# Filler matmuls ahead of the first k^T v, and block 1's q transposed by VectorE

One TensorE program on Trainium2, with a change in two parts. In the opening, six matmuls without a purpose of their own ("filler") are put ahead of the first k^T v, and a second group of filler grows from 7 to 12. At the border between block 0 and block 1, the transposing of block 1's q moves from TensorE to VectorE.

## Chip, cores and metric

One core of one Trainium2 chip. The metric is device time of one execution in microseconds (us). All executions quoted are of the fast state, but for the one of e5, whose state is not known. "Clock" is the granted TensorE clock averaged over a run, 1.000 being full speed; the record counts the time before the first rise as 1.000 too (in the kernel before its first entry is the rise at 22.21 us, and the stretch from 0 to 22.2 reads 1.00). Microseconds read from a trace are of one profiled run of each kernel.

## The reference

```python
def _attn_ref(q, k, v, g_norm):              # q, k, v: (8, 8, 576, 64) float32
    kv = np.einsum('bhsd,bhse->bhde', k, v)  # "k^T v"
    out = np.einsum('bhsd,bhde->bhse', q, kv)  # "q times kv"
    rms = np.sqrt(np.mean(out * out, axis=-1, keepdims=True) + 1e-06)
    return out / rms * g_norm

def _moe_ref(x, w_gate, w_val, w_out):       # x: (4608, 512), d_ff = 1536
    g = x @ w_gate
    silu = g * (1.0 / (1.0 + np.exp(-g)))
    return silu * (x @ w_val) @ w_out

# reference: x = attention output, heads joined, (B*S, H*D); result = _moe_ref(x, ...)
```

## The kernel before

The kernel takes the 4608 tokens in 9 blocks of 512. Each block runs k^T v, q times kv, the norm, up (gate and value), h = silu(g) * value, and down. From block 1 on the large products are computed from sums of sub-blocks that VectorE and GpSimd prepare (`h_sums`, `turn_t`: fewer matmuls, more adding). A scheduler orders each engine's instructions; `tc.issue_after(x)` asks that what is inside be issued behind x.

```python
def load_q(self, i):
    if self.n >= TURNED:                 # TURNED = 3: later blocks load q in quarters
        self.load_quarters(i)
        return
    if self.n == 1:
        tiles = [t_tile().rearrange("p a b -> p (a b)") for _ in range(2)]
    # ... (cut: other blocks' tiles, and the loads)

def turn_q(self, i, pools=None):
    # ...
    if self.n >= TURNED:                 # VectorE transposes
        nc.vector.transpose(out=..., in_=self.q[i])
        return
    for t in (2 * i, 2 * i + 1):         # TensorE transposes, 4 matmuls a tile
        # ... (cut)
        for j in range(NS):
            nc.tensor.transpose(ps[:, j], self.q[t][:, j], ident)

def first(self):                         # block 0
    self.turn_q(0, (b_psum, c_psum))
    self.first_kv()                      # k^T v
    self.product(0)                      # q times kv, first half
    with tc.issue_after(self.multiplied.ins):
        self.turn_q(1, (b_psum, c_psum))
    # ... (cut)
        self.product(1, (b_psum, a_psum))
    self.warm()                          # filler, bridges VectorE's root and scale
    self.root(0, 2)
    self.scale(0)
    # ... (cut)
    self.turn_x(0)
    self.scale(1)

def warm(self):
    ps = c_psum.tile([P, NS, P], F32, name="c")
    for _ in range(7):
        nc.tensor.matmul(ps, lhsT=ident, rhs=self.qt[:, 3], start=True, stop=True)

# the start of the program
blocks[0].load_q(0)
blocks[0].load_first_kv()
blocks[0].load_q(1)
load_weights(4)                          # first four pieces of the weights, 512 KB each
squared, scaled = blocks[0].first()
```

Of the kernel before, what the change touches and what calls it, by code (L numbers as in the profile page):

```python
# [8 lines left out]
F32 = mybir.dt.float32  # L9
# [5 lines left out]
P = 128  # L15
# [3 lines left out]
def kernel(  # L19
# [41 lines left out]
    nc = tc.nc  # L61
# [5 lines left out]
    BLK = P * T  # L67
# [7 lines left out]
    LD = 2 * KT * D  # L75
# [4 lines left out]
    def pool(name, bufs, **kw):  # L80
        return ctx.enter_context(tc.tile_pool(name=name, bufs=bufs, **kw))

    consts = pool("consts", 1)
    ld_pool = pool("ld", 4)
# [14 lines left out]
    ident = consts.tile([P, P], F32, name="ident")  # L99
# [15 lines left out]
    def ring():  # L115

        return r_pool.tile([P, 4, BLK], F32, name="r")

    class Words:
# [12 lines left out]
        def __init__(self, src, shape):  # L132
            self.raw = ld_pool.tile([P, LD], U32, name="ld")[:, 0 : 2 * BLK]
            dst = self.raw.rearrange("p (a b) -> p a b", a=shape[0])
            self.sent = nc.sync.dma_start(out=dst, in_=src)
            self.shape = shape
            self.begun = False
# [55 lines left out]
    class Att:  # L193


        def __init__(self, n):
            self.n = n

            self.cut, half = divmod(n, 2)
            self.split = half * D  # L200
            self.ps, self.z = {}, None
            self.q, self.k, self.v, self.room = [], {}, {}, None
            self.halves = []

        def parts(self, t):

            n, first = self.n, P * t - D * self.n
            if t < self.cut:
                return [(n - 1, S + first, 0, P)]
            if t == self.cut and self.split:  # L210
                return [(n - 1, S - D, 0, D), (n, 0, D, P)]
            return [(n, first, 0, P)]
# [73 lines left out]
            self.q.append(ld)  # L286

        def load_q(self, i):
            if self.n >= TURNED:
                self.load_quarters(i)  # L290
                return
            if self.n == 1:
                tiles = [t_tile().rearrange("p a b -> p (a b)") for _ in range(2)]
            else:
                ld = ld_pool.tile([P, LD], F32, name="ld")
                tiles = [ld[:, 0:BLK], ld[:, BLK : 2 * BLK]]
            for t in range(2):
                tile_ = tiles[t].rearrange("p (h d) -> p h d", h=H)
                for b, s0, p0, p1 in self.parts(2 * i + t):
                    nc.sync.dma_start(  # L300
                        out=tile_[p0:p1], in_=q[b, :, s0 : s0 + p1 - p0, :].rearrange("h p d -> p h d")
                    )
                self.q.append(tile_.rearrange("p (j u) d -> p j (u d)", u=2))
# [21 lines left out]
        def turn_q(self, i, pools=None):  # L325

            if i == 0:
                self.qt = ring().rearrange("p j (t c) -> p t j c", t=T)
            if self.n >= TURNED:
                to = self.qt[:, :, 2 * i : 2 * i + 2].rearrange("p t j c -> p j t c")  # L330
                nc.vector.transpose(out=to.rearrange("p j t c -> p (j t c)"), in_=self.q[i])
                return
            for t in (2 * i, 2 * i + 1):
                pool = pools[t % 2] if pools else m_psum
                ps = pool.tile([P, NS, P], F32, name=pool.name[0])
                for j in range(NS):
                    nc.tensor.transpose(ps[:, j], self.q[t][:, j], ident)
                if t % 2 if self.n == 0 else t:
                    self.copied_q = nc.scalar.copy(out=self.qt[:, t], in_=ps)
                else:  # L340
                    nc.vector.tensor_copy(out=self.qt[:, t], in_=ps)
# [115 lines left out]

        def first(self):
            self.turn_q(0, (b_psum, c_psum))
            self.first_kv()  # L460
            self.product(0)
            with tc.issue_after(self.multiplied.ins):
                self.turn_q(1, (b_psum, c_psum))

            with tc.issue_after(self.copied_q.ins), tc.issue_after(self.summed.ins):
                begun = words[pieces[0]].begin()
            with tc.issue_after(begun.ins):
                self.product(1, (b_psum, a_psum))
            self.warm()
            self.root(0, 2)  # L470
            self.scale(0)
            with tc.issue_after(self.squared.ins), tc.issue_after(self.scaled.ins):
                weights(1)
            self.turn_x(0)
            self.scale(1)
            return self.squared, self.scaled

        def warm(self):

            ps = c_psum.tile([P, NS, P], F32, name="c")  # L480
            for _ in range(7):
                nc.tensor.matmul(ps, lhsT=ident, rhs=self.qt[:, 3], start=True, stop=True)

        def turn(self):
            for i in range(2):
# [42 lines left out]
    TURNED = 3  # L528
# [267 lines left out]
    def t_tile(key=None):  # L796

        stream.held.append(key)
        return t_pool.tile([P, 2, 2 * P], F32, name="t")
# [114 lines left out]
    class Ffn:  # L914
# [49 lines left out]
        def down(self, nxt):  # L964

            down = self.down_
            fill = nxt.steps() if nxt else {}
            for p in (1, 6, 5, 7, 2, 4, 3) if 5 in fill else (1, 5, 6, 7, 2, 4, 3):
                if p == 1:
                    down.turn_t(7, self.ended)  # L970
                if p == 6:
                    down.turn_t(4, nxt.halves[0] if nxt and nxt.n >= TURNED else None)
                down.multiply(p)
                self.make(12)
                if p == 5 and self.n == DEEP - 1:
                    for i in range(2):
                        self.loads(i)
                if p in fill:
                    fill[p]()
                if p == 1:  # L980
                    down.turn_s3()



# [37 lines left out]
    def weights(upto):  # L1022
        nonlocal rounded
        while rounded < min(upto, len(pieces)):
            load_weights(rounded + 4)
            round_w(*pieces[rounded])
            rounded += 1
# [14 lines left out]
    for n in range(NB):  # L1042
        ffn = Ffn(n, blocks[n])
        nxt = blocks[n + 1] if n + 1 < NB else None
# [84 lines left out]
```

## Time and profile before

| kernel before | value |
|---|---|
| time, median of 3 runs | 1037.47 us (1037.41 to 1038.24) |
| span of the profiled run | 1036.2 us |
| TensorE busy | 1014.5 us (98%) |
| VectorE busy | 700.4 us (68%) |
| clock of the profiled run | 1.000 |

TensorE is the bound. So the questions are what TensorE waits for, in which stretch, and at which clock its matmuls run. The lines for that stand in the prediction below. In a timeline, a line has the start, the length, the engine, the line of the kernel, the operation with its tiles, how many records it joins (x72), and in brackets the idle time before it with what ended it.

### The profile page before, as it was taken

How to read it: one execution, taken by the hardware profiler on the slowest of the kernel's cores; microseconds unless marked ns; L12 is line 12 of the kernel's file. 1: busy time of each engine (PE TensorE's matmuls, PEld its weight loads, DVE VectorE, ACT ScalarE, POOL GpSimd, SP SyncE). 2: the span in 40 equal slices, each digit the busy share in tenths (PEclk: the TensorE clock that was granted, in tenths of full speed). 3: DMA queues.
4: the chain of work that ended last, by engine and by line, in shares of the span. 5: the costliest groups of instructions: out<-in, count | busy, mean ns of one | idle time of the engine just before them, and what ended most of it. 6: DMA issues, size and time to landing. Idle time of an engine off the chain costs nothing.

```text
span 1036.2 us, 21446 instructions
## 1 busy us (share of the span) xinstructions
PE 1014.5 (98%) x8586; PEld 904.9 (87%) x8586; DVE 700.4 (68%) x1184; ACT 231.4 (22%) x362; POOL 369.5 (36%) x280
## 2 busy tenths in 40 slices
PE   5999999999999999999999999999999999999998
PEld 4544688778899989998999899988999899989997
DVE  2999596898556856575666666684668566856661
ACT  2665111222212211212111111211212111212110
POOL 0000443435025621563146305640455136512670
PEclk9999999999999999999999999999999999999999
DMA  7689604775468556865686368736862766066601
GB/s 214 200 262 273 140 1 127 186 203 138 130 190 245 120 113 200 240 158 87 195 245 181 61 203 233 212 50 178 247 192 50 171 200 194 22 153 213 191 30 42
DMA packets 247876, 168.15 MB, mean 162 GB/s; under 512 B 124640, under 2 KB 215904, under 8 KB 247776
## 3 DMA queue, kind: packets, MB, share of 16 engines
q1 hardware_dynamic: 221280, 163.36, 56.7%
q10 hardware_dynamic: 26432, 3.41, 2.1%
q8 instruction: 68, 1.11, 0.4%
q14 instruction: 32, 0.26, 0.1%
q0 software_dynamic: 64, 0.00, 0.0%
HBM read 138.02 MB, written 22.41 MB: 155 GB/s over the span
## 4 chain that ended last, share of the span: by engine, by line
PE 91%; DVE 5%; DMA 2%; issue 1%; ACT 1%; POOL 0%; SPq 0%; DVEq 0%; ACTq 0%; POOLq 0%
PE b L700 26%; PE b L551 20%; PE c L700 13%; PE c L551 10%; PE a L700 6%; PE a L551 5%; PE b L994 4%; PE c L994 4%; PE m L316 2%; PE m L357 1%; DVE xi L112 1%; DMA h<-in_v_dram 1%; DVE r L112 1%; DVE t L111 1%; DVE h L112 0%
## 5 line engine op out<-in xcount | busy, mean ns | idle before, releaser
L111 POOL TENSOR_TENSOR r<-r 128x256 f32<-128x256 f32 (+1 forms) x105 | 110.9, 1063 | 308.2 <-DVE r L111 234.3
L111 DVE TENSOR_TENSOR r<-b,r 128x512 f32<-128x512 f32 (+1 forms) x273 | 162.0, 606 | 63.9 <-PE b L700 59.3
L112 POOL TENSOR_TENSOR t<-wo 128x512 f32<-128x512 f32 x81 | 115.6, 1453 | 191.9 <-DVE wo L111 105.4
L111 DVE TENSOR_TENSOR r<-c,r 128x512 f32<-128x512 f32 (+1 forms) x179 | 108.4, 617 | 95.5 <-PE c L700 56.1
L700 PE MATMUL b<-x,t 128*128 128x128 f32 x1092 | 151.0, 275 | 0.0
L700 PEld LDWEIGHTS b<-x,t 128*128 128x128 f32 x1092 | 136.5, 192 | 0.6 <-DVE r L111 0.2
L111 DVE TENSOR_TENSOR r<-a,r 128x512 f32<-128x512 f32 (+1 forms) x99 | 62.5, 631 | 108.7 <-PE a L551 65.8
L113 POOL TENSOR_TENSOR h<-r 128x1024 f32<-128x1024 f32 (+1 forms) x40 | 81.7, 2059 | 88.7 <-DVE r L111 75.6
L700 PE MATMUL c<-xi,t 128*128 128x128 f32 x840 | 112.2, 275 | 0.4 <-DVE xi L111 0.4
L700 PEld LDWEIGHTS c<-xi,t 128*128 128x128 f32 x840 | 102.8, 192 | 0.5 <-DVE xi L111 0.5
L551 PE MATMUL b<-wo,h 128*128 128x256 f32 x432 | 99.4, 382 | 0.1
L551 PE MATMUL b<-t,h 128*128 128x256 f32 x432 | 96.9, 381 | 0.0
L551 PEld LDWEIGHTS b<-t,h 128*128 128x128 f32 x432 | 81.3, 190 | 11.3 <-issue 0.2
L551 PEld LDWEIGHTS b<-wo,h 128*128 128x128 f32 x432 | 79.9, 190 | 12.7 <-DVE h L113 2.5
L714 ACT COPY r<-b 128x512 f32<-128x512 f32 x63 | 36.9, 586 | 212.0 <-PE b L700 200.1
L700 PE MATMUL b<-xi,t 128*128 128x128 f32 x588 | 79.7, 276 | 0.0
L700 PEld LDWEIGHTS b<-xi,t 128*128 128x128 f32 x588 | 72.4, 192 | 0.0
L700 PE MATMUL b<-x,wg 128*128 128x128 f32 x336 | 52.7, 279 | 0.2 <-DVE x L112 0.2
L700 PE MATMUL b<-x,wv 128*128 128x128 f32 x336 | 51.3, 275 | 0.0
L551 PE MATMUL c<-t,s 128*128 128x256 f32 x216 | 48.3, 380 | 0.0
L551 PE MATMUL a<-wo,h 128*128 128x256 f32 x216 | 48.3, 379 | 0.0
L551 PE MATMUL c<-wo,h 128*128 128x256 f32 x216 | 48.1, 379 | 0.0
(136 smaller groups left out, 1579.1 us busy)
## 6 DMA issues: line engine op xcount, KB each, us to landing
t<-w SPq DMA_DIRECT2D x336, 256.0 KB, 3.4
out_dram<-r SPq DMA_DIRECT2D x17, 512.0 KB, 3.1
ld<-in_k_dram SPq DMA_DIRECT2D x26, 288.0 KB, 4.8
ld<-in_v_dram SPq DMA_DIRECT2D x26, 288.0 KB, 5.6
ld<-in_moe_w_gate_dram SPq DMA_DIRECT2D x12, 512.0 KB, 4.7
ld<-in_moe_w_val_dram SPq DMA_DIRECT2D x12, 512.0 KB, 4.6
ld<-in_moe_w_out_dram SPq DMA_DIRECT2D x12, 512.0 KB, 5.1
w<-t SPq DMA_DIRECT2D x18, 256.0 KB, 2.3
```

Source lines behind the costliest of these rows:

```text
L111: add = lambda e, o, a, b: e.tensor_tensor(out=o, in0=a, in1=b, op=OP.add)
L112: sub = lambda e, o, a, b: e.tensor_tensor(out=o, in0=a, in1=b, op=OP.subtract)
L113: mul = lambda e, o, a, b: e.tensor_tensor(out=o, in0=a, in1=b, op=OP.mult)
L316: nc.tensor.matmul(self.kv_ps[r][u * D : (u + 1) * D, g, :], lhsT=k[:, u, c, :], rhs=v[:, u, c, :], start=(c == 0), stop=(c == KT - 1),)
L357: self.multiplied = nc.tensor.matmul(self.ps[i][u][p : p + D, t, j, :], lhsT=self.qt[rows, 2 * i + t, j, p : p + D], rhs=kvs[b % 3][rows, ...
L551: nc.tensor.matmul(banks[e][:, e], lhsT=lhsT, rhs=rhs, start=first and i == 0 and (e == 0 or banks[0] is not banks[1]), stop=i == self.ste ...
L700: nc.tensor.matmul(ps[:, i, f], lhsT=self.weight(o, p, f), rhs=self.operand(o, p), start=first and (i, f) == (0, 0), stop=True, skip_group ...
L714: nc.scalar.copy(out=dst, in_=ps)
L994: nc.tensor.matmul(t, lhsT=w[f // 2][:, i, P * (f % 2) : P * (f % 2 + 1)], rhs=x[:, i, of], start=(i == 0), stop=(i == NS - 1),)
```

## The change

The intent: keep TensorE busy while it waits for k and v, so that it is at full clock when k^T v begins (in the kernel before the clock rose only at 22.21 us, behind k^T v); and take 16 transposes from TensorE at a place where VectorE has time.

```diff
         def __init__(self, n):
+            self.quarters = n == 1 or n >= TURNED
...
         def load_q(self, i):
-            if self.n >= TURNED:
+            if self.quarters:
                 self.load_quarters(i)
                 return
-            if self.n == 1:
-                tiles = [t_tile().rearrange("p a b -> p (a b)") for _ in range(2)]
-            else:
-                ld = ld_pool.tile([P, LD], F32, name="ld")
-                tiles = [ld[:, 0:BLK], ld[:, BLK : 2 * BLK]]
+            ld = ld_pool.tile([P, LD], F32, name="ld")
+            tiles = [ld[:, 0:BLK], ld[:, BLK : 2 * BLK]]
...
-            if self.n >= TURNED:
+            if self.quarters:
                 to = self.qt[:, :, 2 * i : 2 * i + 2].rearrange("p t j c -> p j t c")
-                nc.vector.transpose(out=to.rearrange("p j t c -> p (j t c)"), in_=self.q[i])
+                self.q_turned = nc.vector.transpose(out=to.rearrange("p j t c -> p (j t c)"), in_=self.q[i])
...
         def first(self):
             self.turn_q(0, (b_psum, c_psum))
+            self.warm(6)
             self.first_kv()
             self.product(0)
...
-            self.warm()
+            self.warm(12)
...
-        def warm(self):
+        def warm(self, count):
             ps = c_psum.tile([P, NS, P], F32, name="c")
-            for _ in range(7):
-                nc.tensor.matmul(ps, lhsT=ident, rhs=self.qt[:, 3], start=True, stop=True)
+            for _ in range(count):
+                nc.tensor.matmul(ps, lhsT=ident, rhs=self.qt[:, 0], start=True, stop=True)
...
-                down.multiply(p)
+                with tc.issue_after(nxt.multiplied.ins) if self.n == 0 and p in (5, 6) else ExitStack():
+                    down.multiply(p)
...
                 if p == 1:
-                    down.turn_s3()
+                    with tc.issue_after(nxt.q_turned.ins) if self.n == 0 else ExitStack():
+                        down.turn_s3()
```

## The prediction

> **What bounds the kernel now.** I read the page first, then the waits of TensorE, then the timeline and the chain in the two places that the change touches: the opening (0 to 40 us) and the border of block 0 and block 1 (115 to 126 us).
>
> The busy slices and the waits of TensorE (total, times, longest):
> ```profile
> PE   5999999999999999999999999999999999999998
> ...
> PE b L551 <- ACT r L601: 5.7, 4, 2.3
> PE m L247 <- DMA h<-in_v_dram: 5.6, 2, 4.8
> PE b L337 <- DMA ld<-in_q_dram: 4.2, 1, 4.2
> ```
> TensorE is the bound nearly everywhere: only the first slice is half empty. So a microsecond counts only if it leaves TensorE's own row. The listed waits come to some 17 us of 1036; those on k, v and q belong to the opening.
>
> The opening, timeline of TensorE (start, length, then what it is; L247 is k^T v, L357 q times kv, L482 the existing filler, L404 the turning of x):
> ```profile
> 5.76 1.11 PE L337 MATMUL c<-ident,ld 128*128 128x128 f32 x4 [0.43 <-DMA ld<-in_q_dram]
> 11.72 2.40 PE L247 MATMUL m<-h 64*64 64x64 f32 x72 [4.84 <-DMA h<-in_v_dram]
> 14.91 2.41 PE L247 MATMUL m<-h 64*64 64x64 f32 x72 [0.79 <-DMA h<-in_v_dram]
> 17.92 1.99 PE L357 MATMUL m<-kv,r 64*64 64x64 f32 x64 [0.60 <-DVE kv L111]
> ...
> 23.11 6.28 PE L482 MATMUL c<-r,ident 128*128 128x512 f32 x14
> 29.65 1.06 PE L404 MATMUL m<-ident,r 128*128 128x128 f32 x8 [0.27 <-DVE r L113]
> ```
> k^T v waits for v, which lands in two halves (11.6 and 14.8 us). The filler of 7 matmuls (14 records) bridges the wait for VectorE's root and scale; TensorE goes on at 29.65, 0.27 us after it, released by VectorE. From 39.8 us on it has no gap until block 1.
>
> The same 72 records of k^T v for block 1, and the turning of block 1's q, at 115 us:
> ```profile
> 115.39 1.28 PE L316 MATMUL m<-xi 64*64 64x64 f32 x72
> 116.49 1.25 PE L316 MATMUL m<-ld 64*64 64x64 f32 x72
> 117.67 0.65 PE L337 MATMUL c<-ident,t 128*128 128x128 f32 x4
> 118.16 0.60 PE L337 MATMUL b<-ident,t 128*128 128x128 f32 x4
> 118.59 0.60 PE L337 MATMUL c<-ident,t 128*128 128x128 f32 x4
> 119.03 0.60 PE L337 MATMUL b<-ident,t 128*128 128x128 f32 x4
> 119.47 1.89 PE L551 MATMUL b<-wo,h 128*128 128x256 f32 x8
> ```
> 72 records take 1.1 us here start to start against 2.4 us in the opening, so TensorE runs at half speed there. The records of L357 shorten from 0.31 to 0.22 us at 22.2 us; until then all is slow.
>
> VectorE beside it, and its own transposes of later blocks:
> ```profile
> 115.57 0.69 DVE L113 TENSOR_TENSOR h<-h,c 128x512 f32<-128x512 f32 x1 [6.18 <-PE c L994]
> 116.29 1.76 DVE L111 TENSOR_TENSOR s<-h 128x1536 f32<-128x1536 f32 x1
> 118.09 1.76 DVE L112 TENSOR_TENSOR h<-s,h 128x1536 f32<-128x1536 f32 x1
> ...
> 124.85 1.76 DVE L112 TENSOR_TENSOR h<-h 128x1536 f32<-128x1536 f32 x1 [4.41 <-PE b L551]
> ...
> L331 DVE STREAM_TRANSPOSE r<-ld x12: 1221/1230/1235, 348.6 to 889.7; 128x1024 f32<-128x1024 f32 x12
> ```
> After the sums of h VectorE has 4.41 us free: room for two transposes of 1.23 us.
>
> [...]records of 0.31 us until 22.2 us, 4.3 us after the last gap ended at 17.92, 0.22 us from then on. The page's granted clock reads 1.00 all the while[...]. [...]the quarters move 128 B runs. In the trace later blocks issue such a load every 0.5 us and it lands after 2.0 us (median). [...]at 133.9 us a 128x512 subtract of VectorE beside GpSimd takes 1.76 us, alone 0.68.
>
> **The change, part by part.**
>
> Part 1, block 1's q. Removed from TensorE: 16 transposes, 117.67 to 119.47 = 1.80 us. They stand on the path: TensorE has no gap from 39.8 to 180 us. Added on VectorE: 2 x 1.23 us after the sums of h, 119.85 to 122.2, less a copy of 0.69 that goes. TensorE now goes from k^T v (117.67) straight to the first product of down, 5.2 us, and reaches q times kv at 122.85; VectorE is done at 122.2. The built order puts four matmuls of the second q tile early in it, so both turns are needed, with 0.65 us of slack. The loads: 5 become 32, still 1 MB. Today q's loads issue from 98.8 and land by 111.6. Now they need tiles of the weights' loads, the last read at 101.7, and issue at 0.5 us each: 101 + 16 + 2 = about 119, before the second turn at 121. What follows (block 1's up, where VectorE holds TensorE four times, 5.7 us) starts from events of TensorE, so the shift should carry to the end. After the border the built order of every engine is unchanged. Worth: -1.80.
>
> Part 2, the opening. Six filler matmuls start when the first q copy is done and the transposes are issued, about 6.7 us. One costs 0.86 us at full clock (L482: 0.43 per record, two records), 1.72 at half. The clock rises 4.3 us after work starts by the trace[...]; I take 11.5 us. By then (11.5 - 6.7)/1.72 = 2.8 are done, the other 3.2 take 2.75 us: they end at 14.25. So k^T v starts 2.5 us late, but at full speed: 14.25 + 1.1, then + 1.1 (v's second half is there at 14.8): last end 16.65 against 17.32. Then + 0.6 (kv's copy and add), product(0) 0.95 instead of 1.9, 8 transposes 0.87 instead of 1.9: 19.1 against 21.8. VectorE's chain to x comes with it: about 27.1 instead of 29.5, 2.4 us earlier. But the second filler grows from 7 to 12. In the built order one of them goes ahead of product(1) and 11 behind it: product(1) ends about 20.9, plus 11 x 0.858 = 9.44, makes 30.35. TensorE would then turn x 0.7 us later than today, with x long ready. Of the small waits behind it (0.27, 0.34, 0.20 us) some part goes: full-width work starts perhaps 0.3 us later. Worth: +0.3[...]. The sum of weights that VectorE does earlier is worth nothing, because TensorE is the bound from 40 to 115 us.
>
> Part 3, possible delay of the turns, +0.2 on average (rival B).
>
> Sum: 1037.47 - 1.80 + 0.30 + 0.20 = 1036.2 us.
>
> **Rivals.**
> A. The second filler is no bound, because x is ready only at about 30 us after all (weights of 512 KB landing at 17.8 and 20.5 us, ScalarE's work on them between). Then the opening gains what VectorE's chain gains, up to 2 us: 1034 to 1035. For it: somebody chose 12. Against it: in the chain of waits the span from 21.8 to 29.5 is ScalarE and VectorE alone, no DMA, and it starts with transposes that come 2.7 us earlier.
> B. The turns come late. GpSimd makes nine tiles of wo; today five, then it waits 4.01 us for tiles that hold q, so it is quiet during the first sum of h. Now it isn't stopped, and may meet the sums: each meeting costs VectorE up to 1.1 us. Or the 32 small loads, queued behind k and v loads that take 7 us to land, come at 122 instead of 119. Each would make TensorE wait 0.5 to 1.5 us at q times kv: 1036.7 to 1037.7. Against it: VectorE's weights end about 2 us earlier, so GpSimd starts its nine earlier too.
> C. The gain at the border is swallowed in block 1 by VectorE (busy 19.7 of 20 us at 200 to 240). Then 1037.5 to 1038. Against it: VectorE's work there begins on TensorE's results, and at 160 to 180 it is busy 14 of 20 us.
> D. The filler doesn't lift the clock and runs all cold to 17 us: k^T v late by 5 us, time 1039 or more. Against it: a busy TensorE lifted it once already.
>
> **Range and chances.** [...]B costs up to 1.5, A gives up to 2; runs of one kernel differ by 0.8. Range 1034.6 to 1037.6. Two per cent is 20.7 us; nothing here is of that size, so within 2% nearly surely.
>
> **What would show it.** Right: no transposes by TensorE at 117 us, two of VectorE before q times kv, and no gap of TensorE ahead of it; records of k^T v in block 0 near 0.22 us; a fall to short records between 10 and 14 us; the second filler ending at 30 to 31 us with no wait behind it. Wrong: a wait of TensorE on VectorE's transpose or on q at 123 us (B); a wait after the second filler (A); block 1's wait on ScalarE grown by what was saved (C); k^T v records of 0.31 us (D).

## The result, and the profile after

| | before | after |
|---|---|---|
| time, median | 1037.76 us (1037.41 to 1038.24, 4 runs) | 1044.01 us (1043.26 to 1044.77, 4 runs) |
| ratio | | 1.006 (1.0042 to 1.0077) |
| span of the profiled run | 1036.2 us | 1042.7 us |
| clock, each run | 1.000 (profiled) | 0.997 (profiled), 0.995, 0.995, 0.995 |

Ratios here are the mean time of one kernel's fast runs over that of the other's of the same rounds, so they are not quite the ratio of the medians quoted. The changed kernel is some 6 us slower, within 2% but far outside the predicted range. I followed single TensorE instructions through both traces and noted how much later each starts in the changed kernel. The difference is +4.29 us when the full-width products begin (39.76 us before, 44.05 after), falls to +3.50 behind the border of block 0 and 1, grows by about 2.6 in block 1 and by about 0.6 later.

**The opening.** The waits of TensorE in the changed kernel have a new entry (total, times, longest):

```profile
PE b L550 <- ACT r L600: 6.6, 4, 2.7
...
PE m L355 <- issue: 2.2, 1, 2.2
...
PE m L355 <- DVE r L329: 0.3, 1, 0.3
```

"issue" says that the engine waited for nothing that the profile knows. Its place, in the timeline of TensorE after the change (L481 is the filler, L248 k^T v, L355 q times kv, L335 the turning of q, L402 that of x):

```profile
6.62 6.63 PE L481 MATMUL c<-r,ident 128*128 128x512 f32 x12
13.18 2.49 PE L248 MATMUL m<-h 64*64 64x64 f32 x144
16.43 1.08 PE L355 MATMUL m<-kv,r 64*64 64x64 f32 x57 [0.75 <-DVE kv L111]
19.72 0.49 PE L355 MATMUL m<-kv,r 64*64 64x64 f32 x7 [2.21 <-issue]
20.14 1.11 PE L335 MATMUL b<-ident,ld 128*128 128x128 f32 x4
...
21.91 1.52 PE L481 MATMUL c<-r,ident 128*128 128x512 f32 x2
...
24.45 9.71 PE L481 MATMUL c<-r,ident 128*128 128x512 f32 x22
34.00 1.04 PE L402 MATMUL m<-ident,r 128*128 128x128 f32 x8
```

The first two lines are what the change wanted: k^T v takes 2.49 us for 144 records where it took 2.40 for 72, and q times kv starts at 16.43 instead of 17.92. But after 57 of its 64 records it stands still for 2.21 us. Then the four transposes at 20.14 take 1.11 us, the duration of half clock (four of block 1 at 118.16 us in the kernel before: 0.60). The trace's record of the granted clock has it: up at 9.26, down at 19.50, up again at 22.91. The table by stretches (second column from the left the length, PEclk third from the right) shows the same:

```profile
15.00:20.00 5.00, 2.04 (x106) 1.76 (x98) 0.42 (x1) 0.37 (x1) 0.00 (x0) 0.95 0.90 302
20.00:25.00 5.00, 5.00 (x83) 3.46 (x80) 3.33 (x6) 2.67 (x5) 0.00 (x0) 0.71 0.36 107
```

In the kernel before both stretches read 1.00, though its records are at half clock until 22.2 us: that is the time before the first rise. The filler behind is then about as long as predicted (9.71 us) but starts at 24.45, and ends at 34.16, while VectorE had x ready at 30.27.

What else happens at the stop? The DMA queues' table has a queue for instructions. Two stretches of the changed kernel, from 12 to 17.2 us (first line) and from 17.2 to 18.4 us (second and third; packets, MB, share of 16 engines, which passes 100% where the times of packets overlap):

```profile
q1 hardware_dynamic: 2850, 1.34, 107.0%
...
q1 hardware_dynamic: 390, 0.38, 94.5%
q8 instruction: 1, 0.02, 5.1%
```

Up to 17.2 us all the engines' time goes to the loads of q, k, v and weights. Then one packet of 16 KB of instructions comes: by the trace it starts at 17.28 us and takes 0.98 us. TensorE resumes at 19.72, 1.46 us after its end. Over the whole run there are 68 such packets, and the trace has 17,514 instructions of TensorE (matmuls, weight loads and its own control instructions), 258 for each packet. In the kernel before the packet ran from 17.92 to 18.96, and TensorE, at half clock, came to the instruction with the same number, the 449th, only at 20.75 (17.29 after the change): nothing to see.

**The border.** VectorE and GpSimd in the changed kernel (L111 and L112 on VectorE are the sums of h, L329 the two transposes of q; GpSimd makes tiles of wo):

```profile
120.58 2.81 DVE L111 TENSOR_TENSOR s<-h 128x1536 f32<-128x1536 f32 x1
123.42 2.71 DVE L112 TENSOR_TENSOR h<-s,h 128x1536 f32<-128x1536 f32 x1
126.06 2.36 DVE L329 STREAM_TRANSPOSE r<-ld 128x1024 f32<-128x1024 f32 x2
...
118.05 6.46 POOL L112 TENSOR_TENSOR t<-wo 128x512 f32<-128x512 f32 x4
```

The sums take 2.81 and 2.71 us instead of 1.76 each, the transposes end at 128.42, and TensorE waits 0.34 us for them (the third of the waits above). The lead that the missing transposes gave was 1.70 us at 122 us; 0.90 of it was lost at q times kv, of which the wait is 0.34. So the 1.80 us became 0.79.

**Block 1.** TensorE's four waits on ScalarE are 6.63 us instead of 5.71 by the trace, and behind the last the clock is at half again (244.78 to 248.19): eight records took 1.97 us before, now

```profile
244.12 3.12 PE L550 MATMUL b<-x,t 128*128 128x256 f32 x8 [2.54 <-ACT r L600]
247.04 2.46 PE L550 MATMUL c<-x,wv 128*128 128x256 f32 x8
```

### The profile page after: what moved, and what is told of

It reads as the page before. It is cut to its first block, busy times and chain, and to the rows that moved or that the text cites. A ratio compares the mean times of both kernels' runs of the same rounds, so it can differ in the third digit from the quotient of the medians.

```text
span 1042.7 us, 21481 instructions
## 1 busy us (share of the span) xinstructions
PE 1022.8 (98%) x8592; PEld 906.8 (87%) x8592; DVE 703.7 (67%) x1185; ACT 229.7 (22%) x359; POOL 369.6 (35%) x280
## 3 DMA queue, kind: packets, MB, share of 16 engines
q10 hardware_dynamic: 26432, 3.41, 2.0%
q8 instruction: 68, 1.11, 0.4%
## 4 chain that ended last, share of the span: by engine, by line
PE 82%; DVE 8%; DMA 5%; SPq 1%; issue 1%; ACT 1%; POOL 0%; DVEq 0%; ACTq 0%; POOLq 0%
PE b L699 25%; PE b L550 19%; PE c L699 12%; PE c L550 9%; PE a L699 6%; PE a L550 5%; PE c L481 2%; DMA ld<-in_moe_w_out_dram 2%; PE m L355 1%; DVE r L112 1%; PE m L314 1%; SPq L281 1%; DVE xi L112 1%; DVE r L153 1%; DMA ld<-in_v_dram 1%
## 5 line engine op out<-in xcount | busy, mean ns | idle before, releaser
L111 POOL TENSOR_TENSOR r<-r 128x256 f32<-128x256 f32 (+1 forms) x105 | 110.9, 1062 | 309.5 <-DVE r L111 233.2
L111 DVE TENSOR_TENSOR r<-b,r 128x512 f32<-128x512 f32 (+1 forms) x273 | 161.8, 605 | 64.5 <-PE b L699 58.8
L112 POOL TENSOR_TENSOR t<-wo 128x512 f32<-128x512 f32 x81 | 115.8, 1453 | 192.8 <-DVE wo L111 109.1
L111 DVE TENSOR_TENSOR r<-c,r 128x512 f32<-128x512 f32 (+1 forms) x179 | 108.4, 617 | 94.9 <-PE c L699 55.6
L111 DVE TENSOR_TENSOR r<-a,r 128x512 f32<-128x512 f32 (+1 forms) x99 | 62.4, 631 | 109.4 <-PE a L550 65.8
```

What stands on the lines that cost most here:

```text
L111: add = lambda e, o, a, b: e.tensor_tensor(out=o, in0=a, in1=b, op=OP.add)
L112: sub = lambda e, o, a, b: e.tensor_tensor(out=o, in0=a, in1=b, op=OP.subtract)
```

## The experiments

All runs were correct. There is no e8. "Before" was run beside each group on the same chip: medians 1037.98 us (first group), 1037.39 (second), 1037.60 (third).

| run | what | median us (lowest to highest, runs) | ratio to before |
|---|---|---|---|
| e1 | opening part alone | 1044.68 (1044.56 to 1045.59, 4) | 1.0064 |
| e2 | q part alone | 1038.10 (1037.30 to 1038.91, 4) | 1.0001 |
| e3 | after, second filler 8 | 1039.91 (1038.99 to 1041.14, 4) | 1.0020 |
| e4 | after, GpSimd's last tiles behind the sums | 1047.34 (1045.88 to 1047.71, 4) | 1.0088 |
| e5 | after, first filler in narrow pieces | 1045.59 (1 run) | |
| e6 | after, first weights later | 1038.14 (1038.06 to 1039.14, 4) | 1.0009 |
| e7 | e6 with second filler 8 | 1036.30 (1035.12 to 1037.84, 4) | 0.9989 |
| e9 | e7 without the q part | 1036.03 (1034.88 to 1036.93, 18) | 0.9983 |
| e10 | e7, weights later still | 1036.23 (1034.69 to 1038.52, 20) | 0.9988 |
| e11 | before, first weights later | 1037.28 (1036.70 to 1038.55, 12) | 0.9997 |

### e1 and e2: which part

The opening part alone: block 1's q as before.

```diff
-            self.quarters = n == 1 or n >= TURNED
+            self.quarters = n >= TURNED
...  # and block 1's tiles for q, and the plain order of down, as in the kernel before
```

> The opening's part of the change alone (fillers 6 and 12), block 1's q loaded and turned as before. Theory: the opening costs 4.3 us by itself, because the second filler holds TensorE until 34.0 us while x is ready at about 30.4, and that goes through to the end: 1042 us. If the loss of 2.6 us in block 1 (longer waits, a stretch at half clock at 245 us) belongs to the opening too, 1044 to 1045. Rival (the loss comes from q in quarters): 1037 to 1038.

The q part alone: the opening as before.

```diff
-            self.warm(6)
             self.first_kv()
...
-            self.warm(12)
+            self.warm(7)
...  # and rhs=self.qt[:, 3] again in warm
```

> Block 1's q in quarters and turned by VectorE alone; the opening as before (one filler of 7). Theory: TensorE saves 1.80 us of transposes but waits about 1.0 us because GpSimd's tiles of wo hold up VectorE's sums of h (2.8 instead of 1.76 us each): 1036.8 to 1037. The prediction's own sum for this part: 1035.9. Rival (block 1's loss of 2.6 us comes with this part): 1039 to 1040.

Measured: 1044.68 us for the opening part, 1038.10 for the q part (ratio 1.0001, 0.9986 to 1.0016). The opening explains the whole loss; it has the same stop after 57 records (19.16 to 21.90 us) and half clock behind it. The time is that of the second expectation (1044 to 1045), but not by its path: in e1's trace the clock rose at 12.07 us instead of 9.26 and the full-width products began 6.62 us late, while block 1 lost only 0.7 and never fell to half clock. Four traces with the 12 fillers pair up by the clock's rise: up at 9.26 and 9.44 us (the changed kernel, e4), the full-width products are 4.29 and 4.50 us late; up at 12.07 and 12.25 (e1, e5), 6.62 and 7.00. So the opening's loss in one trace is no exact size.

The q part is worth nothing at the end, though TensorE is 2.06 us ahead of the kernel before at 120 us, of which 0.36 is from the opening. It loses that in block 1: it is 1.77 us ahead at 195 us and 0.5 at the end, and the four waits on ScalarE add up to 6.98 us instead of 5.71. That is rival C of the prediction. At the border VectorE is slowed here too:

```profile
115.93 2.20 DVE L111 TENSOR_TENSOR s<-h 128x1536 f32<-128x1536 f32 x1
118.16 2.71 DVE L112 TENSOR_TENSOR h<-s,h 128x1536 f32<-128x1536 f32 x1
```

but here TensorE has no listed wait at q times kv (it loses 0.29 us there), against the 1.0 us of wait that I had expected; and the time is above the theory's 1036.8 to 1037 and below the rival's 1039.

### e3: too much filler

```diff
-            self.warm(12)
+            self.warm(8)
```

> The whole change, the second filler with 8 instead of 12 matmuls. Theory: the filler ends 4 x 0.858 = 3.4 us earlier, at about 30.6 us, about when x is ready (30.4): the time falls by 3.4 us to 1040.6. Rival (x is not ready either, or the wait for it costs the clock): no change or slower than 1043.

Measured: 1039.91 us, 4.1 under the changed kernel's median. In this run the stop was 3.01 us (after 57 records again), and yet the filler ended at 33.33, 0.45 us behind x. So the changed kernel's filler held TensorE up for about as long as four of its matmuls take (4 x 0.86 = 3.4 us). What is left above the kernel before is the stop and the half clock, since x itself is late.

### e4: GpSimd kept away from the sums

```diff
-            self.h_sums(0, NP, nc.vector)
+            self.ended = self.h_sums(0, NP, nc.vector)
             self.down_ = Down(self)      # turn_t(7) then waits for self.ended
```

> The whole change, GpSimd's six later tiles of wo kept back until the sums of h are done. Theory: the two sums take 1.76 us each again, the turns end before TensorE needs them, its waits at q times kv (0.27 and 0.6 us) go: 1043.0 to 1043.2. Rival (q's small loads or the turns themselves are late): the waits stay, 1044.

Measured: 1047.34 us, 3.3 over the changed kernel and outside both expectations. The sums are back to 1.76 us and the wait for the transposes is gone, which shows that the wait came from the meeting of the two engines:

```profile
120.80 1.76 DVE L111 TENSOR_TENSOR s<-h 128x1536 f32<-128x1536 f32 x1
122.59 1.76 DVE L112 TENSOR_TENSOR h<-s,h 128x1536 f32<-128x1536 f32 x1
...
155.37 1.14 PE L402 MATMUL m<-ident,r 128*128 128x128 f32 x8 [2.90 <-DVE r L113]
```

But GpSimd's tiles now come later and meet other work of VectorE (two instructions at 131 to 133.4 us take 1.17 and 1.19 us instead of 0.17); x of block 1 is late by 2.90 us, and half clock follows that wait (156.22 to 159.63). A removed meeting of 2 us came back as a larger one.

### e5: does the stop belong to the instruction count?

The theory by then: TensorE stops where the instructions that it holds end, and waits for the 16 KB packet. In the changed kernel and in e1, e3 and e4 it stops behind its 449th instruction (matmuls, weight loads and its own control instructions counted in order). The rival: it belongs to q times kv.

```diff
             for _ in range(count):
-                nc.tensor.matmul(ps, lhsT=ident, rhs=self.qt[:, 0], start=True, stop=True)
+                for j in range(NS) if count == 6 else (slice(0, NS),):
+                    nc.tensor.matmul(ps[:, j], lhsT=ident, rhs=self.qt[:, 0, j], start=True, stop=True)
```

> The changed kernel with its first filler cut into 24 matmuls of 128 columns instead of 6 of 512: the same work of the array, but 72 more instructions of TensorE (a float32 matmul takes two weight loads and two matmuls). Theory (instruction fetch): TensorE stops where the instructions that it holds end, the 449th, so it stops again, but after about 21 of the 64 records of block 0's q times kv instead of 57, near 16.5 to 17 us, and the 16 KB packet of instructions falls before the resumption by about 1.4 us. Rival (the stop belongs to q times kv itself, to its banks or to the power): the stop is again after 57 of 64 records, or is gone. The time is not the question; 1042 to 1046 us under either.

Measured, timeline of TensorE:

```profile
7.03 8.01 PE L482 MATMUL c<-r,ident 128*128 128x128 f32 x48
...
18.22 0.56 PE L355 MATMUL m<-kv,r 64*64 64x64 f32 x21 [0.75 <-DVE kv L111]
21.71 0.93 PE L355 MATMUL m<-kv,r 64*64 64x64 f32 x43 [2.93 <-issue]
```

The stop is after 21 of the 64 records, as said: 72 more instructions move it by 36 records (a record has its weight load: 8592 of each in the changed kernel's trace, and 14 of each for the 7 filler matmuls of the kernel before). The packet ran from 19.11 to 20.16, and TensorE resumed 1.55 us later. The moment was missed: the clock rose only at 12.25 us in this run, so everything came nearly 2 us later than I wrote. The rival is out.

### e6: does the packet wait behind the loads?

```diff
             self.first_kv()
+            load_weights(4)              # taken from the start of the program
+            for x in pieces[0:4]:        # each waits for the last matmul of k^T v
+                tc.add_manual_dep(words[x].sent.ins, self.last_kv.ins.name, ...)
             self.product(0)
```

> The changed kernel with the first four loads of weights (2 MB) held back until the last matmul of block 0's k^T v, so that fewer bytes are queued ahead of the 16 KB packet of instructions that starts at 17.28 us in the changed kernel. Theory (the fetch waits behind the loads): the packet starts by about 16 us, the stop in q times kv is under 1 us, the clock doesn't fall at 19.5 us, and the kernel is 1 to 2.5 us faster than the changed one, 1041.5 to 1043 us, still limited by the second filler. Rival (the fetch comes a fixed time after its trigger): the stop stays at 2 to 3 us and the time within 0.7 us of the changed kernel's, or above it where weights come late.

Measured, timeline of TensorE (L487 is the filler):

```profile
16.67 1.08 PE L355 MATMUL m<-kv,r 64*64 64x64 f32 x57 [0.73 <-DVE kv L111]
17.99 0.34 PE L355 MATMUL m<-kv,r 64*64 64x64 f32 x7 [0.23 <-issue]
...
21.23 9.71 PE L487 MATMUL c<-r,ident 128*128 128x512 f32 x22
30.78 1.04 PE L402 MATMUL m<-ident,r 128*128 128x128 f32 x8
```

The packet starts at 15.44 us, the stop is 0.23, the clock doesn't fall (the four transposes at 18.75 us take 0.60, the time of full clock), the second filler begins at 21.23 instead of 24.45, and the time is 1038.14 us: 5.9 less (5.3 by the ratios to the kernel before), and more than I had said. Of that, 3.2 us are the opening (full-width work at 40.87 instead of 44.05). The rest comes in block 1: a fall of the clock at 200.30 us put TensorE 1.3 us behind the kernel before, and by 228 us all but 0.1 of it was made up, mostly because two of the four waits on ScalarE shrank (0.60 us to nothing, 0.93 to 0.59).

The packet's delay can be read in all traces from a fixed point, the execution of the 180th TensorE instruction (chosen afterwards; with every tenth one from the 60th to the 310th the two groups stay apart). With the weights loaded at the start it begins 2.8 to 3.8 us later (before, after, e1 to e5); with the weights held 0.9 to 1.7 us (e6, e7, e9, e10, e11).

### e7, e9 and e10: the repaired kernel, with and without the q part

e7 is e6 with `self.warm(8)`.

> As the run with late weights, and the second filler 8 matmuls instead of 12 (3.4 us less at full clock). Theory: without the stop and the half clock the 12 would end at about 30.5 us, and x would be ready near 27 to 28; 8 of them end at about 27, so x is turned near 28, 1 to 2 us earlier than in the kernel before, and the whole takes 1036 to 1038 us. If the stop stays, the time is that of the run with 8 fillers alone, 1039 to 1041 us.

e9 is e7 with block 1's q as in the kernel before (the edit of e1).

> The opening part of the change alone (q of block 1 as in the kernel before), with the first weights held until the end of k^T v and 8 matmuls in the second filler. Theory (the opening's loss was the stop for instructions, the half clock after it and 4 fillers too many): 1.5 to 2 us earlier at 40 us than the kernel before, as with both parts repaired, and so 1035.5 to 1036.5 us where block 1 gives nothing back. Rival (what is gained in the opening is given back in block 1 too, because something there doesn't move with TensorE): 1037 to 1038 us.

e10 holds the weights until a quarter of q times kv is done.

```diff
-                    words[x].sent.ins, self.last_kv.ins.name, ...
+                    words[x].sent.ins, self.early.ins.name, ...   # 8th of product(0)'s 32 matmuls
```

> Both parts, 8 matmuls in the second filler, and the first weights held a little longer, until a quarter of block 0's q times kv is done (about 17 us instead of 16). The packet of instructions then has the queues for itself between v and the weights. Theory: it starts by 15.5 us and the stop is under 0.4 us in every run (with the hold at the end of k^T v it was 0.23 in one and 0.81 us in the other), the time 0 to 0.6 us under that of the kernel with the hold at the end of k^T v, 1035.5 to 1036.5. Rival: the stop stays at 0.8 us, or weights come late and x is ready after 28 us: 1036.5 to 1038.

Measured: 1036.30, 1036.03 and 1036.23 us. e9 is 0.9983 of before (0.9976 to 0.9990), e10 0.9988 (0.9982 to 0.9995), e7 0.9989 (0.9974 to 1.0004). All three are in the predicted range of the change. e9, timeline of TensorE (L490 is the filler, L405 the turning of x):

```profile
17.00 1.35 PE L358 MATMUL m<-kv,r 64*64 64x64 f32 x64 [0.75 <-DVE kv L111]
...
21.25 6.28 PE L490 MATMUL c<-r,ident 128*128 128x512 f32 x14
27.36 1.06 PE L405 MATMUL m<-ident,r 128*128 128x128 f32 x8
```

No stop that the timeline lists (the 450th instruction starts 0.14 us after the 449th), x turned at 27.36 instead of 29.65, and about 2.2 us ahead of the kernel before from there to block 1 and through it (1.9 at 198 us, 2.0 at 240); 0.7 is lost later, at a wait of 0.63 us for a weight load at 717 us, and 1.3 is left at the end. So what is gained in the opening is not given back in block 1: the rival in e9's expectation is out. e10's stop was 0.42 us in its profile, against 0.23 and 0.81 with the earlier hold; the bound of 0.4 that I had set was just missed, and its time is that of e7 within the scatter.

The q part adds nothing on top: e10 was 3.9 us ahead at 120 us, 3.1 at 198, 2.0 at 240 and 1.4 from 243 on. The last step is a fall of the clock behind a wait of 1.91 us (237.20 to 240.62). Other runs have a lowered clock too, though a mean does not say where: 16 of e10's 20 runs have a mean clock below 1.000, their mean time is 1036.7 us, that of the other four 1035.6; of e9's 18 runs 7 are below 1.000, and their times differ by 0.2 only. That is a correlation; I made no kernel that keeps the clock up in block 1.

### e11: the control

The kernel before with the edit of e6.

> The kernel before with nothing changed but the first weights held until the end of k^T v. Theory (at half clock TensorE comes to the 449th instruction only when the packet is there): no stop with either order of loads, so nothing is gained: 1037 to 1038 us. Rival (holding the weights helps in itself, by a lighter load on the queues, and not through the packet of instructions): faster than before by 1 us or more.

Measured: 1037.28 us, ratio 0.9997 (0.9989 to 1.0005). Holding the weights brings v 1.2 us earlier in the profile (k^T v starts at 10.53 instead of 11.72), but by the medians the kernel gains 0.3 us (by the interval, from 1.1 gained to 0.5 lost), against more than 5 us in e6. The profiled run, the fastest of the twelve (1036.70 us), kept a lead of 1.1 us from 40 us to the end. So e6's gain is not, or for about a fifth at most, a lighter load on the queues in itself.

## Why the prediction was wrong

**Right.** Part 2's course up to q times kv: k^T v was to start at 14.25 and did at 13.18, at full clock; the last end was to be 16.65 and was 15.68. Rival D is out. That k^T v came even earlier than predicted was luck of the clock: it rose at 9.26 us and not at 11.5, which was my estimate (the filler's start at 6.7 and the 4.3 us of the kernel before make 11.0), and in the nine kernels with the first filler it rose between 8.51 and 12.25. (Two sums of the prediction are off: 14.25 + 1.1 + 1.1 is 16.45, and two turns of 1.23 us from 119.85 end at 122.3. The granted clock that reads 1.00 all the while in the kernel before does show half clock once the clock has been up, 0.95 and 0.71 above.) The length of the second filler behind product(1) (9.44, measured 9.71). VectorE's x at 27.1 us once the stop is gone (27.20 in e6). Part 1's mechanism: no TensorE transposes, two of VectorE, and rival B's meeting with GpSimd, which I had named and sized at up to 1.1 us for each sum (measured 1.05 and 0.95).

**The step that failed** is this one of part 2: "Then + 0.6 (kv's copy and add), product(0) 0.95 instead of 1.9, 8 transposes 0.87 instead of 1.9: 19.1 against 21.8." It takes for granted that an engine with its data and a full clock runs. The runs showed a stop of 2.21 us: TensorE, faster by then (144 records of k^T v in 2.49 us against 72 in 2.40), had started its 449th instruction at 17.29, and the packet that began at 17.28 landed at 18.26. That it had run out of the instructions it held, and that the next 16 KB waited behind 512 KB loads, is my reading of e5 (72 instructions more, the stop 36 records earlier) and e6 (those loads held: the packet at 15.44, the stop 0.23). In the stop the clock fell, to half from 19.50 to 22.91; in e6 it did not fall there. The transposes ended at 22.1 and product(1) at 24.5 instead of 19.1 and 20.9. From "makes 30.35" (x turned) it is 3.65 us to the measured 34.00: 2.21 of the stop, and some 1.5 of the half clock (from the resumption to the second filler's main part 4.73 us, in e6 3.24). What is left cancels: q times kv began 0.8 us earlier than predicted, and the way from there to x is 0.8 us longer than predicted even in e6, its stop left out.

**What half clock had hidden.** I priced the half clock of the kernel before at 2.7 us (19.1 against 21.8). Most of that was no cost: its packet ended at 18.96, TensorE went past the 449th instruction at 20.75, and in the eight runs that stopped there 1.3 to 1.6 us passed between the packet's end and the resumption. By that, an estimate, TensorE could have come to this place 0.2 to 0.5 us earlier, not 2.7, without moving the packet.

**The mis-sized terms.** Part 2 was put at +0.3 and was +4.29 (up to +7.00 where the clock rose later, in e5). With the stop repaired and 12 fillers it is +1.1 (e6), because x was turned 1.1 us later and not 0.7, and the small waits ahead of the full-width work didn't shrink. That 12 was too many was in the prediction (0.7 us); with x delayed to 30.27 by the stop they overshot by 3.9 us. Part 1, -1.80, was -0.79 at the border and nothing at the end (e2; e9 against e7 and e10): rival C, to which I gave too little weight because block 1 "starts from events of TensorE". It does, but VectorE is busy there 19.7 of 20 us, and a TensorE that came early alone only waited longer (on ScalarE 6.98 us in e2, 5.71 before). The opening of e9, which brings all engines forward, kept its gain through block 1.

**Open.** Why TensorE resumes only some 1.5 us after the packet's end (1.46 in the changed kernel, 1.55 in e5). Which gaps bring the clock down: in the changed kernel it fell at gaps of 2.21 us (17.51 to 19.72) and 2.54 (241.59 to 244.12), each time to half for 3.41 us, and not at one of 2.68 (201.83 to 204.51); in the kernel before it stayed up through gaps of 2.33 (198.34 to 200.67) and 1.85 (237.87 to 239.72). And whether the clock in block 1 is what takes the q part's last microsecond.

## What to carry to other kernels

Before speeding up TensorE near the start of a kernel, look in the trace where its instruction packets land and how full the DMA queues are then. Here a TensorE at half clock reached its 449th instruction at 20.75 us, 1.79 behind the packet's end at 18.96, and the faster one was there at 17.29, 0.97 ahead of it (18.26); "issue" behind the 449th instruction, for 2.2 to 3.0 us in five kernels, was the sign. Holding back four loads of weights that weren't needed yet turned +6 us into -1.6 us here, with 8 fillers and without the q part. Here a lead of TensorE alone (2.06 us in e2) was mostly lost in a stretch that VectorE bounds, and a lead of all engines (2.1 us in e9) passed it.
